# An attention, gated-convolution and feed-forward kernel on one core: new load order, nine opening products, one ring of five accumulator banks, and a new instruction list

## The chip, the core and the metric

The program runs on one core of a Trainium2 chip. The core has five engines with their own instruction streams: TensorE (PE in the profile, with its weight loads as PEld), VectorE (DVE), ScalarE (ACT), GpSimd (POOL) and SyncE (SP), which here only issues transfers. Each engine takes its instructions in the order in which they were written; between engines, semaphores order the work. The metric is device time in microseconds (us) of one execution, as a median over runs.

## The reference, cut to what matters

```python
# q, k, v: (2, 8, 768, 64); attention with a window of +-15 positions and 24 block summaries
k_sum = k.reshape(B, H, nb, 32, D).max(axis=3)          # 24 blocks of 32 keys: maximum
v_sum = v.reshape(B, H, nb, 32, D).mean(axis=3)         # and mean of the values
scores_l = where(|i - j| < 16, scale * q @ k.T, -1e9)
scores_s = scale * q @ k_sum.T + log(32)
a = softmax(concatenate([scores_l, scores_s]))
x = a @ concatenate([v, v_sum])                          # -> (2, 768, 512)
h = relu(x @ w_in)                                       # 512 -> 1024
gate = sigmoid(conv3(h, conv_w))                         # along the sequence, by channel
x = (h * gate) @ w_out                                   # 1024 -> 512
xn = (x - mean) / sqrt(var + 1e-6) * g_ln
out = x + relu(xn @ w_ch1) @ w_ch2                       # 512 -> 2048 -> 512
```

The weights arrive as 64-bit floats. They are loaded as raw 32-bit words and narrowed on the chip in three steps (`...z` on VectorE, `...b` on ScalarE, `...c` on VectorE), then split into a high part (`...d`, ScalarE) and a remainder (`...e`, GpSimd), because the big products are made as three reduced-precision products: high by high, high by low, low by high.

## The kernel before

The program is a list of 1850 operations, each a small function that emits a few instructions. `plan.op` declares an operation with the engines that it may run on, what it comes after, and what it takes from a ring of buffers. The string `ORDER` names all operations by number in the order in which they are emitted, with the letter of the chosen engine (V, A, G, P, S); so it decides both the order on every engine and which engine does a movable operation. The numbers of nanoseconds in `plan.op` are only notes for whoever made the list: they emit nothing.

The work in order of time:

- **Attention** over 12 pairs j of 64-row windows (6 per batch). For a pair, `M` writes a mask into two banks of scores (units 2j and 2j+1), `S{j}` adds the products of queries and keys, `X` takes the row maximum (VectorE), `E` the exponentials (ScalarE, four ACTIVATE instructions), `Q` and `R` the reciprocal of the row sums, `N` the normalisation (GpSimd or VectorE), `P` the transposes, `C` their copy out, `T{j}` the value products, and `H{j}`, `L{j}` the copy of the result into a high and a low part of `xT`. Before that, keys and queries are transposed (`kt`, `kb`, `qt`), copied out (`kn`, `qe`), and the block maxima of the keys taken (`kmb`). The scores of the first batch need the maxima of all three blocks of 256 keys (`k0`, `k1`, `k2`), which `kc` copies into the key tiles.
- **The gated convolution** in 48 steps i: `h{i}` are 12 products (a group of 8 steps for each 256 rows), `r` the relu (ScalarE, it frees the bank of h), `b`, `c` the convolution, `t`, `g` the gate, `u`, `v` its high and low part (ScalarE, GpSimd), and `x{i}` six products, up to about ten steps behind h. The first of them, `h0`, waits for `L0`, `L1` and, through two columns that `xh1` copies, `L2`.
- **The feed-forward part**: `ch` (12 products) and `ac` (three products each into six accumulators), over both batches, about from 215 us to the end.

TensorE writes into eight banks of an accumulator memory (PSUM). `PS` divides them until the attention is through: tag `tr` 2 banks (transposes), `sc` 2 (scores), `av` 1 (value products), `h` 1, `x2` 2 (x, and in the opening also key transposes and block means of v). A tag is a ring: a request gets the bank of the request that lies as many requests back as the ring is long, and waits until that one is read out.

```python
PS = {"tr": (ps_a, 2), "sc": (ps_a, 2), "av": (ps_a, 1), "h": (ps_m, 1), "x2": (ps_m, 2)}
```

All loads are issued by SyncE in list order. The opening order before: conv weights, a block of `w_in`, `k2`, `w_in`, `k1`, `k0`, `w_in`, `q0`, two blocks of `w_in`, `q1`, and so on; each block of k, q, v, and weights is 512 KB. The program begins with six products on a zeroed tile (`warm_up`) whose result nobody reads.

## Time and profile before

| | |
|---|---|
| median of three runs | 497.84 us (497.32 to 498.03) |
| the profiled execution | 497.72 us, span 496.0 us from the first to the last instruction |
| TensorE busy | 478.9 us, 97% of the span |
| VectorE, ScalarE, GpSimd busy | 306.5, 225.7, 149.6 us |
| granted TensorE clock, mean | 1.00 |

The page shows TensorE busy in nine tenths or more of every fortieth of the span but the first three (6, 8 and 8 tenths), the fourth (7) and the last (6). VectorE is at nine tenths or nearly so in the first six slices, and the transfers fill the first eight. In the second half VectorE, ScalarE and GpSimd are mostly idle and TensorE never is. Bars of this kind tell where an engine has room; they don't tell what the program's end hangs on, which is read from the waits.

### The profile page before, as it was taken

How to read it: one execution, taken by the hardware profiler on the slowest of the kernel's cores; microseconds unless marked ns; L12 is line 12 of the kernel's file. 1: busy time of each engine (PE TensorE's matmuls, PEld its weight loads, DVE VectorE, ACT ScalarE, POOL GpSimd, SP SyncE). 2: the span in 40 equal slices, each digit the busy share in tenths (PEclk: the TensorE clock that was granted, in tenths of full speed). 3: DMA queues.
4: the chain of work that ended last, by engine and by line, in shares of the span. 5: the costliest groups of instructions: out<-in, count | busy, mean ns of one | idle time of the engine just before them, and what ended most of it. 6: DMA issues, size and time to landing. Idle time of an engine off the chain costs nothing.

```text
span 496.0 us, 8646 instructions
## 1 busy us (share of the span) xinstructions
PE 478.9 (97%) x3342; PEld 417.3 (84%) x3342; DVE 306.5 (62%) x600; ACT 225.7 (46%) x601; POOL 149.6 (30%) x183
## 2 busy tenths in 40 slices
PE   6887999999999999999999999999999999999996
PEld 4646888888889888887999898998899889998985
DVE  4998989877677898999999931251463011410114
ACT  3897978666755586755453402340153001110110
POOL 4776555634643244415432000330044000000000
PEclk9999999999999999999999999999999999999999
DMA  8999998201110225000635000422022000300003
GB/s 253 347 261 258 240 180 161 60 1 34 30 34 1 88 85 169 1 1 9 213 119 163 8 0 1 170 86 85 1 87 83 0 1 0 128 0 2 0 1 127
DMA packets 60136, 43.26 MB, mean 87 GB/s; under 512 B 34324, under 2 KB 55088, under 8 KB 60096
## 3 DMA queue, kind: packets, MB, share of 16 engines
q1 hardware_dynamic: 59952, 42.58, 31.2%
q8 instruction: 26, 0.43, 0.4%
q14 instruction: 14, 0.11, 0.1%
q10 hardware_dynamic: 144, 0.13, 0.1%
HBM read 39.22 MB, written 3.15 MB: 85 GB/s over the span
## 4 chain that ended last, share of the span: by engine, by line
PE 81%; DVE 6%; DMA 6%; SPq 2%; ACT 2%; issue 1%; POOL 1%; DVEq 0%; ACTq 0%; POOLq 0%
PE ch L1112 27%; PE acc L1147 26%; PE h L704 10%; PE x L776 10%; PE av L489 2%; DMA s_k<-in_k_dram 2%; DVE c L732 2%; DMA vw<-in_v_dram 2%; PE sc L473 1%; PE tr L567 1%; DMA raw<-in_moe_w_ch_dram 1%; PE tr L351 1%; DMA early<-in_k_dram 1%; SPq L662 1%; DVE g L745 1%
## 5 line engine op out<-in xcount | busy, mean ns | idle before, releaser
L1147 PE MATMUL acc<-wh,ch 128*128 128x512 f32 x382 | 126.2, 394 | 0.7 <-ACT x2b L252 0.7
L1123 DVE SCALAR_TENSOR_TENSOR ch<-ch,ch 128x384 fp32r<-128x384 f32 x64 | 35.1, 555 | 133.7 <-ACT ch L1119 133.6
L1112 PE MATMUL ch<-xnT,wh 128*128 128x384 f32 x512 | 99.8, 336 | 0.0
L1119 ACT ACTIVATE ch<-ch 128x384 fp32r<-128x384 f32 x64 | 30.8, 491 | 150.5 <-PE ch L1112 101.8
L1112 PEld LDWEIGHTS ch<-xnT,wh 128*128 128x128 f32 x512 | 90.6, 188 | 3.5 <-DVE ch L1123 0.2
L1147 PEld LDWEIGHTS acc<-wh,ch 128*128 128x128 f32 x382 | 71.6, 188 | 16.4 <-ACT x2b L252 1.1
L704 PE MATMUL h<-xT,wi 128*128 128x258 f32 x576 | 82.9, 288 | 1.2 <-ACT h L716 1.1
L704 PEld LDWEIGHTS h<-xT,wi 128*128 128x128 f32 x576 | 75.5, 189 | 9.1 <-ACT h L716 5.9
L645 POOL TENSOR_TENSOR wl<-raw,wh 128x512 fp32r<-128x512 f32 x32 | 43.0, 1364 | 117.9 <-ACT wh L643 94.0
L1147 PE MATMUL acc<-wl,ch 128*128 128x512 f32 x191 | 75.0, 393 | 0.0
L776 PE MATMUL x<-wo,ghi 128*128 128x512 f32 x192 | 61.5, 401 | 0.0
L763 POOL TENSOR_TENSOR glo<-g,ghi 128x256 fp32r<-128x256 f32 x48 | 39.7, 836 | 62.7 <-ACT ghi L756 52.8
L732 DVE SCALAR_TENSOR_TENSOR c<-h,ccol,c 128x256 f32<-128x256 f32 x96 | 51.2, 544 | 7.9 <-POOL c L256 4.6
L1112 PE MATMUL ch<-xnT,wl 128*128 128x384 f32 x256 | 54.9, 336 | 0.0
L1112 PEld LDWEIGHTS ch<-xnT,wl 128*128 128x128 f32 x256 | 45.3, 188 | 0.0
L1147 PEld LDWEIGHTS acc<-wl,ch 128*128 128x128 f32 x191 | 35.8, 188 | 6.7
L776 PE MATMUL x<-wo,glo 128*128 128x512 f32 x96 | 37.9, 394 | 0.0
L1082 DVE STREAM_TRANSPOSE xf<-xn 32x384 f32<-32x384 f32 x64 | 36.4, 569 | 1.2
L776 PEld LDWEIGHTS x<-wo,ghi 128*128 128x128 f32 x192 | 32.3, 189 | 4.1 <-issue 0.3
L538 ACT ACTIVATE prob<-sc,nm 128x120 f32<-128x120 f32 x96 | 33.2, 370 | 2.7 <-DVE nm L526 2.7
L643 ACT CAST wh<-raw 128x512 fp32r<-128x512 f32 x32 | 19.9, 662 | 24.0 <-PE acc L1147 13.7
L628 ACT ACTIVATE raw<-raw 128x512 f32<-128x512 f32 x32 | 20.6, 677 | 17.8 <-DMA raw<-in_moe_w_ch_dram 17.8
(129 smaller groups left out, 584.1 us busy)
## 6 DMA issues: line engine op xcount, KB each, us to landing
raw<-in_moe_w_ch_dram SPq DMA_DIRECT2D x32, 512.0 KB, 4.8
wst<-in_moe_w_out_dram SPq DMA_DIRECT2D x8, 512.0 KB
vw<-in_v_dram SPq DMA_DIRECT2D x20, 192.0 KB, 4.7
wst<-in_moe_w_in_dram SPq DMA_DIRECT2D x5, 512.0 KB
s_q<-in_q_dram SPq DMA_DIRECT2D x8, 256.0 KB, 6.5
early<-in_k_dram SPq DMA_DIRECT2D x3, 512.0 KB, 8.0
x2a<-in_moe_w_in_dram SPq DMA_DIRECT2D x3, 512.0 KB
early<-in_v_dram SPq DMA_DIRECT2D x3, 512.0 KB, 6.1
```

The source lines that it names most:

```text
L538: A.activation(out=pr[:, p, :], in_=sc[:, p * NK:(p + 1) * NK], func=AF.Exp, bias=nm[:, p:p + 1], scale=1.0, accum_out=sm[:, p:p + 1])
L628: A.activation(out=f, in_=f, func=AF.Prelu, scale=F64_SCALE, alpha=F64_SIGN)
L645: lambda e: G.tensor_tensor(out=lo(), in0=narrowed(raw()), in1=hi().bitcast(F32), op=ALU.subtract),
L704: T.matmul(live["h", i][:, 0:CH + 2], w_[:, c, f * 128:(f + 1) * 128], x_[:, c, :], start=(k_ == 0 and c == 0), stop=(k_ == 2 and c == 3))
L732: V.scalar_tensor_tensor(out=ct, in0=ht[:, kk:kk + CH], scalar=ccol[:, kk * NF + f:kk * NF + f + 1], in1=ct, op0=ALU.mult, op1=ALU.add)
L763: on[e].tensor_tensor(out=glo, in0=live.pop(("g", i)), in1=live["ghi", i].bitcast(F32), op=ALU.subtract)
L776: T.matmul(x2ps[g, t], l[:, ts_], r[:, f, :], start=(f == 0 and j == 0), stop=(f == NF - 1 and j == 2))
L1082: V.transpose(out=o_, in_=i_)
L1112: T.matmul(cp[:, 0:384], w_[:, c * 128:(c + 1) * 128], x_[:, c, s], start=(n_ == 0), stop=(n_ == 11))
L1119: A.activation(out=chs[b, m][0][:, s], in_=live[key][:, 0:384], func=AF.Relu)
L1123: V.scalar_tensor_tensor(out=lo[:, s], in0=live.pop(key)[:, 0:384], scalar=0.0, in1=hi[:, s].bitcast(F32), op0=ALU.max, op1=ALU.subtract)
L1147: T.matmul(acc[key], l[:, ts_], r[:, 512:1024], start=(mm == 0 and j == 0), stop=(done and j == 2))
```

## The change

Six things change; what the kernel computes stays. (1) `ORDER` is a new list, so nearly every engine's order moves, and 87 operations move to another engine: among them 10 normalisations `N` go from GpSimd to VectorE and 2 the other way, 4 query copies from ScalarE to VectorE and 4 back, 3 key copies from ScalarE to VectorE. (2) The first loads are `k0`, `k1`, `k2`, then a block of `w_in`, the conv weights, `w_in`, `q0`, two of `w_in`. (3) `warm_up` has nine products in place of six. (4) The banks `tr`, `sc` and `av` become one ring `tr` of five. (5) The h of odd steps up to 11 takes its bank from that ring too, so that consecutive h have different banks. (6) The release of the attention's memory waits for these relus as well (`HR`); they lie far ahead of it. The changed nanosecond notes emit nothing.

```diff
-4G 0V 8S 61S 12S 73S 11S 1P 178G 228G 3G 2G 10S 52V 157G 53A 6G 54V 7G 67S 63A 62V 5G 64V 13S 36P 79S 33P 37A 75A
...
+1834P 1845V 1846P 1849V 1847V
...
-    PS = {"tr": (ps_a, 2), "sc": (ps_a, 2), "av": (ps_a, 1), "h": (ps_m, 1), "x2": (ps_m, 2)}
+    PS = {"tr": (ps_a, 5), "h": (ps_m, 1), "x2": (ps_m, 2)}
...
-        for _ in range(6):
+        for _ in range(9):
...
-            tag = SCT.get(u, "sc")
+            tag = "tr"
...
-            av = live["av", j] = bank("av")
+            av = live["av", j] = bank("tr")
...
-        ex.give.append((SCT.get(i, "sc"), ("s", i)))
+        ex.give.append(("tr", ("s", i)))
...
+        htag = "tr" if i % 2 and i < 12 else "h"
...
-                    live["h", i] = bank("h")
+                    live["h", i] = bank(htag)
...
-    lk = {n: dma(f"lk{n}", 1456, load_pairs("k", k, 0, n, early_at(0, n))) for n in range(3)}
+    lk = {n: dma(f"lk{n}", 1650, load_pairs("k", k, 0, n, early_at(0, n))) for n in range(3)}
...
-    gate2 = list(XL.values())
+    gate2 = list(XL.values()) + HR
```

TensorE's order in the opening. Ahead of these rows stand the six, now nine, opening products. `L358` are transposes of keys and queries (in `before` k2, k1, k0, then q0 and q1), `L465` (now `L464`) the masks, `L473` (`L472`) the score products, 32 for a pair, `L821` (`L823`) the block means of v, `L567` (`L566`) the transposes of the probabilities. Before, from the key transposes on:

```order
L358 MATMUL x_195<-ident,early_83 64x128 x8
L358 MATMUL x_210<-ident,early_83 64x128 x8
L358 MATMUL tr<-ident,early_83 64x128 x16
L358 MATMUL x_250<-ident,early_83 64x128 x8
L358 MATMUL tr<-ident,early_83 64x128 x8
L473 MATMUL sc<-kw_86,qb_89 64x120 x16
L358 MATMUL tr<-ident,early_84 64x128 x16
L821 MATMUL x_338<-early_84,ind 24x512 x2
```

And now:

```order
L358 MATMUL x_254<-ident,early_83 64x128 x8
L358 MATMUL tr<-ident,early_83 64x128 x8
L472 MATMUL tr<-kw_86,qb_89 64x120 x32
L823 MATMUL x_332<-early_84,ind 24x512 x2
L848 MATMUL x_346<-ident,crow 128x28
L823 MATMUL x_332<-early_84,ind 24x512 x2
L566 MATMUL tr<-ident,prob 120x128 x8
L823 MATMUL x_332<-early_84,ind 24x512 x2
L358 MATMUL tr<-ident,early_84 64x128 x16
```

Before, the first pair's scores (`S0`, whose equal instructions the view counts as x16) stand alone, and q1 is transposed right behind them; now four masks are written early and `S1` and `S0` stand together (x32), with the transposes of q1 (`early_84`, 16) behind the first two probability transposes. What stands before `h0` is the same set of TensorE operations in both lists.

ScalarE's order from the first exponentials (`L538`, now `L537`) on. `L628`/`L643` (`L627`/`L642`) are the narrowing and the high part of a block of weights, `L252` copies out of banks. Before:

```order
L538 ACTIVATE prob,sm<-sc,nm 128x120 x8
L628 ACTIVATE wst<-wst 128x512
L628 ACTIVATE x2a<-x2a 128x512
L643 CAST wi_81<-wst 128x4x128
L643 CAST wi_81<-x2a 128x4x128
L628 ACTIVATE wst<-wst 128x512
L538 ACTIVATE prob,sm<-sc,nm 128x120 x8
L252 COPY probT<-tr 120x512
L252 ACTIVATE vsum<-x_338 24x512
```

And now:

```order
L537 ACTIVATE prob,sm<-tr,nm 128x120 x4
L642 CAST wi_81<-wst 128x4x128
L537 ACTIVATE prob,sm<-tr,nm 128x120 x8
L627 ACTIVATE x2a<-x2a 128x512
L642 CAST wi_81<-x2a 128x4x128
L627 ACTIVATE wst<-wst 128x512
L252 COPY probT<-tr 120x512
L252 ACTIVATE vsum<-x_332 24x512
L537 ACTIVATE prob,sm<-tr,nm 128x120 x4
```

Three of the first four exponentials now come together and the fourth after three weight steps and two copies; from the first exponential to the copy `H2` that `h0` needs, ScalarE has 8 exponentials, 8 weight steps and 9 copies before, and 8, 12 and 11 now.

## Rows read from the trace of the kernel before

**Rows 1.** Stretches: busy PE, PEld, DVE, ACT, POOL; clock, DMA share, GB/s.

```profile
0.00:10.00 10.00, 5.94 (x36) 3.97 (x38) 3.26 (x7) 3.45 (x5) 4.70 (x25) 1.00 0.79 242
...
30.00:40.00 10.00, 7.47 (x118) 4.59 (x117) 9.91 (x21) 8.68 (x34) 7.77 (x7) 1.00 1.19 200
...
300.00:350.00 50.00, 50.00 (x256) 45.68 (x255) 13.80 (x24) 14.20 (x26) 10.36 (x8) 1.00 0.25 85
```

**Rows 2.** What TensorE waited for, longest first: us in total, times, longest.

```profile
PE x L358 <- DMA early<-in_k_dram: 3.0, 1, 3.0
PE tr L567 <- POOL prob L557: 2.3, 3, 1.4
PE av L489 <- DVE parts L951: 1.4, 1, 1.4
PE sc L465 <- ACT prob L538: 1.3, 3, 0.8
PE sc L473 <- ACT kw L252: 1.2, 1, 1.2
PE h L704 <- ACT h L716: 1.1, 2, 0.9
...
PE acc L1147 <- ACT x2b L252: 0.7, 1, 0.7
PE tr L351 <- DMA s_k<-in_k_dram: 0.6, 1, 0.6
```

**Rows 3.** Timeline of TensorE's opening: start, duration, operation, wait before it.

```profile
1.04 2.74 PE L277 MATMUL h<-warm 128*128 128x512 bf16 x6 [1.04 <-DVE warm L272]
...
6.79 1.97 PE L358 MATMUL x<-ident,early 128*64 128x128 f32 x16 [3.01 <-DMA early<-in_k_dram]
...
8.53 1.95 PE L358 MATMUL tr<-ident,early 128*64 128x128 f32 x16
...
16.65 1.09 PE L358 MATMUL tr<-ident,early 128*64 128x128 f32 x16
...
18.93 1.05 PE L473 MATMUL sc<-kw,qb 64*64 64x120 f32 x32 [1.19 <-ACT kw L252]
...
25.38 1.05 PE L473 MATMUL sc<-kw,qb 64*64 64x120 f32 x32
```

**Rows 4.** Timeline of the other engines in the opening.

```profile
0.79 0.42 SPq L791 DMA_DIRECT2D craw<-in_moe_conv_w_dram  x1
...
1.27 0.41 SPq L662 DMA_DIRECT2D wst<-in_moe_w_in_dram  x1
...
5.20 0.69 ACT L628 ACTIVATE wst<-wst 128x512 f32<-128x512 f32 x1 [2.48 <-DMA wst<-in_moe_w_in_dram]
...
15.92 1.28 DVE L379 TENSOR_REDUCE ksum<-tr 128x16 f32<-128x512 f32 x2
```

**Rows 5.** Timeline of ScalarE from its first exponential.

```profile
22.19 0.36 ACT L538 ACTIVATE prob<-sc,nm 128x120 f32<-128x120 f32 x1
...
23.55 0.37 ACT L538 ACTIVATE prob<-sc,nm 128x120 f32<-128x120 f32 x1
...
37.00 1.12 ACT L252 COPY probT<-tr 120x512 f32<-120x512 f32 x2
...
45.47 0.59 ACT L252 CAST xT<-av 128x512 fp32r<-128x512 f32 x1
45.96 1.28 ACT L628 ACTIVATE wst<-wst 128x512 f32<-128x512 f32 x2
```

**Rows 6.** Timeline of TensorE: the first h.

```profile
47.50 1.72 PE L704 MATMUL h<-xT,wi 128*128 128x258 f32 x12
```

**Rows 7.** GpSimd beside VectorE, then L633's durations (ns: least, median, longest).

```profile
13.89 1.56 POOL L645 TENSOR_TENSOR wi<-wst,wi 128x512 fp32r<-128x512 f32 x1 [0.72 <-ACT wi L643]
14.55 1.45 DVE L633 SCALAR_TENSOR_TENSOR wst<-wst 128x512 uint32<-128x512 uint32 x1 [0.25 <-ACT wst L628]
...
L633 DVE SCALAR_TENSOR_TENSOR wst<-wst x13: 666/690/1451, 5.9 to 80.6; 128x512 uint32<-128x512 uint32 x13
```

More of the change, by code (lines that the diff above doesn't have):

```diff
@@ L275, in warm_up @@
         wb = bank("h")
-        for _ in range(6):
+        for _ in range(9):
             T.matmul(wb.rearrange("p (a b) -> p a b", a=4), warm, warm.unsqueeze(1).to_broadcast([128, 4, 128]),
                      start=True, stop=True)
-    w0_ = plan.op("warm", (("P", 2990),), warm_up, [wz], take=[("h", "warm")])
+    w0_ = plan.op("warm", (("P", 3843),), warm_up, [wz], take=[("h", "warm")])
     w0_.give.append(("h", "warm"))
@@ L490, in f_av @@
                                  ps[a][:, p, 64 * h_:64 * h_ + 64], start=True, stop=True)
-        tt = T_[j] = plan.op(f"T{j}", (("P", 1090),), f_av, cs + [LV[j], LVS[j]], take=[("av", j)])
+        tt = T_[j] = plan.op(f"T{j}", (("P", 1090),), f_av, cs + [LV[j], LVS[j]], take=[("tr", ("av", j))])
         for a in range(2):
@@ L666, in weight @@
         prev = j - 6 if j in (6, 7, 8) else j - 3 if j > 8 else None
-        l = dma(f"lw{j}", 1456, ld, WD[prev] if prev is not None else [])
+        l = dma(f"lw{j}", 1800, ld, WD[prev] if prev is not None else [])
         if j < NF:
@@ L707, in m_step @@
                            ([waits[0]] + waits[2:] if k_ < 2 else waits) + [prev],
-                           take=[("h", i)] if k_ == 0 else [])
+                           take=[(htag, ("h", i))] if k_ == 0 else [])
         H_[i] = prev
@@ L790, in local_summary_attention_moe_kernel @@
     craw = at.tile([24, 256], F32, name="craw")
-    lc = [dma("lc0", 70, lambda: nc.sync.dma_start(out=craw.bitcast(U32),
+    lc = [dma("lc0", 300, lambda: nc.sync.dma_start(out=craw.bitcast(U32),
                                                    in_=conv_w.rearrange("k (f p) -> (k f) p", p=256))),
           dma("lc1", 10, lambda: nc.sync.dma_start(out=crow[24:28], in_=g_ln.rearrange("(c p) -> c p", p=128)))]
-    lk = {n: dma(f"lk{n}", 1456, load_pairs("k", k, 0, n, early_at(0, n))) for n in range(3)}
-    lq = {0: dma("lq0", 1456, load_pairs("q", q, 0, 0, early_at(0, 3))),
-          1: dma("lq1", 1456, load_pairs("q", q, 0, 1, early_at(1, 3)))}
-    lvp = {n: dma(f"lvp{n}", 1456, load_pairs("v", v, 0, n, early_at(1, n))) for n in range(3)}
+    lk = {n: dma(f"lk{n}", 1650, load_pairs("k", k, 0, n, early_at(0, n))) for n in range(3)}
+    lq = {0: dma("lq0", 1650, load_pairs("q", q, 0, 0, early_at(0, 3))),
+          1: dma("lq1", 1650, load_pairs("q", q, 0, 1, early_at(1, 3)))}
+    lvp = {n: dma(f"lvp{n}", 1650, load_pairs("v", v, 0, n, early_at(1, n))) for n in range(3)}
     for n in range(NCH):
@@ L895, in f @@
             stage["q", m] = t
-        return dma(f"lq{m}", 2912, f, take=[("s_q", m)])
+        return dma(f"lq{m}", 2700, f, take=[("s_q", m)])
     def k_keep(m, ld):
@@ L945, in ld @@
                                       :, hf * 1024:(hf + 1) * 1024])
-            l = dma(f"lvb{i}", 1092, ld, take=[("s_k", ("vb", i))])
+            l = dma(f"lvb{i}", 1850, ld, take=[("s_k", ("vb", i))])
             def f(e, i=i, raw=raw):
@@ L1207, in local_summary_attention_moe_kernel @@
     with tc.manual_schedule():
-        plan.trace(list(XL.values()))
+        plan.trace(gate2)
         ps_a.release()
```

186 lines of the change are left out of this document (94 added, 92 removed).

## The prediction, on record before the run

> **What bounds the kernel now.** I read the stretches first. Late in the program TensorE is busy 50.00 of 50 us [rows 1]: there only its own work counts, and the change alters no count of it outside the warm-up. Early it is different: from 30 to 40 us TensorE is busy 7.47 of 10 while VectorE has 9.91 and ScalarE 8.68 [rows 1]. So the attention's start is bound by the two engines that read the banks out, and TensorE waits for what they finish.
>
> The list of TensorE's waits says how much there is to win [rows 2]: 3.0 us for the first keys, then 2.3, 1.4, 1.3 and 1.2 behind normalisation, value sums, exponentials and key columns, and 1.1, 0.7 and 0.6 for the bank of h, the copy of the last x and a late key load. That is 11.6 us in all. The opening of TensorE shows the first keys at 6.79, the first pair's scores at 18.93 and the second pair's at 25.38 [rows 3]; ScalarE begins its exponentials at 22.19 [rows 5]; the first h comes at 47.50 [rows 6]. Both lists have the same TensorE operations ahead of the first h. So the end moves by two things alone: the time at which the first h starts, and the waits behind it.
>
> **The opening, step by step.** The end of the profiled execution is 497.72 us, 1.72 beyond its span of 496.0 and 0.12 below the median, 497.84.
>
> *Keys.* The first weight block was issued at 1.27 and was there at 5.20 [rows 4], 3.93 later; `k2`, behind it, was there at 6.79 [rows 3], 1.6 later. `k0` is now issued first, at the 0.79 of the conv weights [rows 4], so it lands at about 4.7, and `k1` at 6.3. Nine opening products take 1.5 times the 2.74 us of six [rows 3] and end at about 5.0: they fill the wait, and cost 0 to 0.3 us. TensorE starts on keys 1.8 us earlier.
>
> *Pace of TensorE.* Sixteen transposes took 1.97 and 1.95 us at 6.79 and 8.53, and 1.09 at 16.65 [rows 3]. This is the slower of the two levels (1.2 GHz) and then the faster (2.4 GHz), although the granted clock stands at 1.00 for 0 to 10 us [rows 1]; ahead of the slow ones TensorE had stood idle for 3.0 us. With the gap filled, the faster level may come earlier: between nothing and 0.9 us on each of the blocks behind the first. I count half of one block, since VectorE takes over next. The Trainium skill (TensorE: Matmul & The Clock Gate, Part 1) says that the clock is throttled by default and that activity releases it. By that page all blocks but the first would run at the faster level, and what VectorE then sees is some 1 us earlier; no run here has shown it.
>
> *VectorE to the first scores.* From the end of the second sixteen transposes, at about 5.0 + 1.95 + 1.5 = 8.4, VectorE's list has nine whole-bank operations (five maxima, two key copies, two query copies) and eight smaller ones (two weight blocks, the conv weights, the key columns). Two maxima take 1.28 [rows 4], so nine take 5.8; for the smaller ones I take an estimate of 0.5 us each, the largest being 0.69 [rows 7], so 4.0. With 0.5 for two waits on TensorE the scores can start at 18.7, range 17.7 to 19.2. That is where the first pair was (18.93), but now both pairs run, the second 6 us earlier than at 25.38 [rows 3].
>
> *ScalarE to the first h.* Two maxima follow weights and key edges, about 3 us after the scores' start; the first exponential begins at 21.7 where it was 22.19 [rows 5]. From there to the copy `H2` ScalarE has 8 exponentials of 1.36 (22.19 to 23.55), 12 weight steps of 0.64 (two in 1.28) and 11 copies of 0.56 (two in 1.12) [rows 5]: 10.9 + 7.7 + 6.2 = 24.8 us. Before it was 10.9 + 5.1 + 5.0 = 21.0, in the 23.9 us from 22.19 to the end of `H2` at 46.06 [rows 5]; 2.9 us were waits. So four weight steps and two copies have moved ahead of `H2`, and eat what the denser start gives. With no wait at all `H2` ends at 46.5, with as many waits as before at 49.4. I take 0.5 us of waits, because the exponentials of two pairs are ready together: 47.0. Before, 1.44 us lay between `H2` and h (46.06 to 47.50); with the same, the first h starts at **48.4, 0.9 us later** than now (range 47.0 to 50.5). VectorE's four normalisations ahead of that point lie inside this, unless they are stretched (below).
>
> **Behind the first h.** A later h moves everything behind it one for one. What can be won back is in the waits there [rows 2]: 1.1 for h's bank, 0.7 in front of the first accumulation, 0.6 for the key load, and perhaps 0.4 of the 1.3 of scores.
> - 0.7: the new list puts three `ch` (36 products) between the last x and the first accumulation, so the copies that it waited for are covered. I count all of it.
> - 0.6: `k4` is now loaded first of the second batch's keys, and fewer value rows stand ahead of it. All of it.
> - 1.1: the bank that alternates is lent only up to step 11, and these waits can fall at any step. I count half, 0.55.
> Moved operations elsewhere (the convolution's steps between engines, key edges between VectorE and GpSimd) lie under TensorE's work; with that cover gone each would cost its own 0.2 to 0.8 us once. The five-bank ring costs nothing by itself.
>
> **Sum.** 497.72 + 0.9 - 0.7 - 0.6 - 0.55 = 496.8, less 0.1 for the scores' wait: **496.7 us**. What a measurement of this kernel can tell from no change is about 0.2%, 1.0 us: 496.84 to 498.84.
>
> **Rivals.**
> - *A full gain.* If the faster clock comes at once and ScalarE waits for nothing, the first h starts at 47.0, 0.5 earlier, and all 2.4 us behind it go: 497.72 - 0.5 - 2.4 = 494.8; with the other score waits 494.3. For it: ScalarE's 2.9 us of waits before came from serial pairs. Against: it has 3.8 us more work there.
> - *No change.* The opening is 0.9 later and the late waits change place: with half of 2.4 us won, 497.4, with none 498.6. For it: in the late stage VectorE is still needed for each step, and the list gives it more.
> - *Slower: the ring's order.* In one ring a request waits for the request five back. The second query transpose of q1 gets the bank of the first pair's masks, which is read out only by `E0`, now the fourth exponential; behind it on TensorE stand the probability transposes and `S2`, `S3`. I have `E0` end at 31; each us later moves `S2`, the next exponentials and the first h by a us. If `E0` is 2.5 us late, the first h is at 50.9, and the end is 497.72 + 3.4 - 1.4 = 499.7. It decides from about 1.5 us on. For it: `E0` is behind a maximum that is behind a normalisation and a weight step on VectorE, each waiting for another engine. Against: the others of this ring are free in time by my sums.
> - *Slower: normalisations on VectorE.* A VectorE operation with two operands from the data memory, begun at 14.55 beside GpSimd's of 13.89 to 15.45, took 1.45 where the median is 0.69 [rows 7]. The four normalisations now on VectorE ahead of `L2` meet GpSimd's weight steps; at up to 0.76 each they cost up to 3.0, half of it on the path: 498.2. The Trainium skill (SBUF, Who interferes with whom) gives the rule: VectorE instructions with two inputs there are blocked by a GpSimd instruction that reads it, for its whole length. This row agrees in part: the longest was lengthened by 0.76, not by the full 1.56.
> - *The opening products miss.* If `k0` lands at 5.7, not 4.7, the gap returns and 0.5 to 1 us is lost: 497.4. It is within the case of no change.
>
> **Chances.** My forecast with its own spread (495.6 to 497.8) 0.42; full gain 0.14; no change or a missed warm-up 0.18; the ring's order 0.16; the normalisations 0.10. Faster by over 0.2%: about 0.6 of the forecast and all of the full gain, 0.40. Slower: the ring, and 0.4 of the normalisations and of no change, 0.28. Same 0.32. The range of 8 in 10 leaves out the best of the full gains and the worst of the ring: 494.2 to 500.2.
>
> **What would show each step.** Right: the first key transposes at 4.7 to 5.1 with no wait for `k`; sixteen transposes at about 1.1 us from the third block on; the first scores, 64 products together, at 17.7 to 19.2; the first exponential at 21 to 22.3; the first h at 47 to 50; the 0.7 before the first accumulation and the 0.6 for the key load gone. Wrong: a wait of a us or more of the q transposes for `E0`; normalisations on VectorE above 1 us; new waits of TensorE for VectorE between 190 and 230, where the late list is tight.

## The result: slower, and the profile after

The changed kernel took **503.84 us** (median of four runs, 502.24 to 504.76) where the kernel before took 497.93 in the same comparison (497.32 to 498.76): a ratio of **1.011, 95% interval 1.0073 to 1.0146**. The forecast was 496.7, in a range of 494.2 to 500.2. The profiled execution took 504.22 us, with a span of 502.5 and a mean granted clock of 0.99.

What TensorE waited for, longest first (us in total, times, longest); the rows answer to [rows 2]:

```profile
PE tr L566 <- POOL prob L556: 6.1, 2, 4.3
PE tr L472 <- DVE qb L256: 2.9, 1, 2.9
PE h L704 <- ACT h L716: 2.6, 4, 1.2
PE acc L1149 <- ACT ch L1121: 1.5, 2, 1.3
...
...
PE acc L1149 <- DVE ch L1125: 0.7, 1, 0.7
```

The waits that the prediction counted as gone are gone: 3.0 for the first keys, 0.7 for the copy of the last x, 0.6 for the late key load. What it didn't see stands in their place: 2.9 and 4.3 in the opening, 2.6 where 1.1 was for the bank of h, and 2.2 of `acc` for the relu of `ch`, where there was none.

TensorE's timeline, which answers to [rows 3] and [rows 6]:

```profile
5.24 1.09 PE L358 MATMUL tr<-ident,early 128*64 128x128 f32 x16 [0.29 <-POOL mask_l L294]
...
17.35 2.57 PE L472 MATMUL tr<-kw,qb 64*64 64x120 f32 x64 [2.92 <-DVE qb L256]
19.85 2.83 PE L823 MATMUL x<-early,ind 128*24 128x512 f32 x4
...
26.48 1.23 PE L566 MATMUL tr<-ident,prob 128*120 128x128 f32 x8 [1.80 <-POOL prob L556]
...
33.91 1.05 PE L472 MATMUL tr<-kw,qb 64*64 64x120 f32 x32
...
41.15 1.11 PE L566 MATMUL tr<-ident,prob 128*120 128x128 f32 x4 [4.31 <-POOL prob L556]
...
43.04 1.98 PE L488 MATMUL tr<-probT,vw 120*64 120x64 f32 x32
...
51.13 1.70 PE L704 MATMUL h<-xT,wi 128*128 128x258 f32 x12 [0.82 <-POOL xT L254]
```

The opening is as forecast down to the first scores, and even earlier: keys at 5.24, the fast pace at once (1.09 for sixteen), scores at 17.35. Then the gain is lost. The third pair's scores (`S2`, 33.91) stood at 31.59 before:

```profile
31.59 1.05 PE L473 MATMUL sc<-kw,qb 64*64 64x120 f32 x32
```

and the first h at 51.13 is 3.6 us later than in [rows 6]. On the way some operations take nearly twice their time: the fifth pair's probability transposes 1.11 (four took 0.65 elsewhere), 32 value products 1.98 (1.15 before). The stretches show why (busy PE, PEld, DVE, ACT, POOL; clock, DMA share, GB/s):

```profile
18.40:21.70 3.30, 3.30 (x35) 1.62 (x28) 3.20 (x7) 1.37 (x6) 1.19 (x1) 0.50 1.12 358
...
38.90:45.60 6.70, 4.45 (x43) 4.01 (x44) 4.64 (x14) 5.04 (x24) 2.46 (x3) 0.50 0.97 293
```

The granted clock, 1.00 through all of [rows 1], falls to 0.50 twice, each time around an idle stretch of TensorE: after the wait of 2.92 that ends at 17.35, and during the 4.31 that end at 41.15. That is the slower of the two levels, 1.2 instead of 2.4 GHz. The 1.00 of [rows 1] for 0 to 10 us is not a measured clock: the trace's first record of it is a rise to 1.00, at 12.09 us in the kernel before and at 4.70 now, and the view counts the time ahead of the first record as 1.00. The transposes of 1.97 in [rows 3] lie before that rise.

Behind the first h, the same view for three stretches, after and then before:

```profile
60.00:90.00 30.00, 29.28 (x288) 24.40 (x287) 28.93 (x55) 24.17 (x68) 19.26 (x22) 1.00 0.73 161
90.00:250.00 160.00, 158.24 (x1274) 138.03 (x1273) 142.97 (x305) 100.89 (x295) 61.72 (x76) 1.00 0.19 55
250.00:340.00 90.00, 87.65 (x435) 77.62 (x434) 51.08 (x89) 27.73 (x52) 16.20 (x12) 1.00 0.22 70
```

```profile
60.00:90.00 30.00, 29.40 (x244) 25.45 (x243) 27.23 (x54) 23.48 (x59) 16.57 (x21) 1.00 0.86 163
90.00:250.00 160.00, 158.16 (x1266) 138.09 (x1265) 136.41 (x294) 100.92 (x292) 68.87 (x84) 1.00 0.19 58
250.00:340.00 90.00, 90.00 (x454) 81.21 (x453) 51.58 (x91) 28.92 (x54) 16.13 (x13) 1.00 0.25 82
```

From 60 to 250 us TensorE idles as long as before (0.7 and 1.8 against 0.6 and 1.8): the waits that went were replaced. From 250 to 340 it never idled; now it idles 2.35 us. So the 6.5 us between the two profiled executions are **3.6 at the first h and 2.4 between 250 and 340 us**, with 0.5 elsewhere. That is one execution of each. The late part isn't a constant of the list: in eight other runs whose order is the same from 250 to 340 us, TensorE idled 0.6 to 1.8 us there (*six_products* 1.84, *vr2_gpsimd* 0.99, *fill_three* 0.82).

Two of these late waits, in the timelines of VectorE, TensorE, SyncE and ScalarE:

```profile
287.90 1.29 DVE L632 SCALAR_TENSOR_TENSOR raw<-raw 128x512 uint32<-128x512 uint32 x2 [0.39 <-ACT raw L627]
289.11 0.55 DVE L1125 SCALAR_TENSOR_TENSOR ch<-ch,ch 128x384 fp32r<-128x384 f32 x1
...
289.71 0.72 PE L1149 MATMUL acc<-wh,ch 128*128 128x512 f32 x2 [0.69 <-DVE ch L1125]
...
328.88 0.37 SPq L1044 DMA_DIRECT2D raw<-in_moe_w_ch_dram  x1
...
335.87 1.20 ACT L627 ACTIVATE raw<-raw 128x512 f32<-128x512 f32 x2 [1.02 <-DMA raw<-in_moe_w_ch_dram]
336.98 0.47 ACT L1121 ACTIVATE ch<-ch 128x384 fp32r<-128x384 f32 x1
...
337.50 0.51 PE L1149 MATMUL acc<-wh,ch 128*128 128x512 f32 x1 [1.30 <-ACT ch L1121]
```

The relu of `ch` (`ca` on ScalarE, L1121; `cv` on VectorE, L1125) is written behind the narrowing of a weight block (L627, L632). The narrowing waits for its transfer or for its neighbour, the relu waits behind it in the queue with its operand long there, and the next accumulation waits for the relu.

### The profile page after: what moved, and what is told of

It reads as the page before. It is cut to its first block, busy times and chain, and to the rows that moved or that the text cites. A ratio compares the mean times of both kernels' runs of the same rounds, so it can differ in the third digit from the quotient of the medians.

```text
span 502.5 us, 8642 instructions
## 1 busy us (share of the span) xinstructions
PE 481.1 (96%) x3345; PEld 417.1 (83%) x3345; DVE 314.4 (63%) x615; ACT 223.7 (45%) x599; POOL 139.6 (28%) x170
## 4 chain that ended last, share of the span: by engine, by line
PE 66%; DVE 14%; DMA 7%; issue 5%; POOL 4%; ACT 2%; SPq 0%; DVEq 0%; POOLq 0%; ACTq 0%
PE acc L1149 21%; PE ch L1114 20%; PE x L778 9%; PE h L704 9%; DMA raw<-in_moe_w_ch_dram 6%; DVE xf L1084 3%; PE tr L488 2%; POOL wl L644 2%; DVE c L734 2%; PE tr L472 2%; PE tr L566 2%; DVE wst L632 1%; DVE raw L623 1%; DVE raw L632 1%; DMA early<-in_k_dram 1%
## 5 line engine op out<-in xcount | busy, mean ns | idle before, releaser
L1125 DVE SCALAR_TENSOR_TENSOR ch<-ch,ch 128x384 fp32r<-128x384 f32 x64 | 35.3, 555 | 130.8 <-ACT ch L1121 130.6
L1121 ACT ACTIVATE ch<-ch 128x384 fp32r<-128x384 f32 x64 | 31.0, 489 | 149.8 <-PE ch L1114 96.7
L704 PE MATMUL h<-xT,wi 128*128 128x258 f32 x504 | 72.3, 287 | 3.4 <-ACT h L716 2.6
L704 PEld LDWEIGHTS h<-xT,wi 128*128 128x128 f32 x504 | 66.1, 189 | 10.1 <-ACT h L716 6.1
L734 DVE SCALAR_TENSOR_TENSOR c<-h,ccol,c 128x256 f32<-128x256 f32 x96 | 54.4, 582 | 3.4 <-ACT c L252 1.7
L537 ACT ACTIVATE prob<-tr,nm 128x120 f32<-128x120 f32 x96 | 33.3, 371 | 6.8 <-DVE nm L525 5.3
L627 ACT ACTIVATE raw<-raw 128x512 f32<-128x512 f32 x32 | 20.6, 678 | 28.5 <-DMA raw<-in_moe_w_ch_dram 28.5
L642 ACT CAST wh<-raw 128x512 fp32r<-128x512 f32 x32 | 20.1, 660 | 18.0 <-PE acc L1149 9.2
```

The lines of the kernel that those rows point to most:

```text
L537: A.activation(out=pr[:, p, :], in_=sc[:, p * NK:(p + 1) * NK], func=AF.Exp, bias=nm[:, p:p + 1], scale=1.0, accum_out=sm[:, p:p + 1])
L627: A.activation(out=f, in_=f, func=AF.Prelu, scale=F64_SCALE, alpha=F64_SIGN)
L704: T.matmul(live["h", i][:, 0:CH + 2], w_[:, c, f * 128:(f + 1) * 128], x_[:, c, :], start=(k_ == 0 and c == 0), stop=(k_ == 2 and c == 3))
L734: V.scalar_tensor_tensor(out=ct, in0=ht[:, kk:kk + CH], scalar=ccol[:, kk * NF + f:kk * NF + f + 1], in1=ct, op0=ALU.mult, op1=ALU.add)
L1121: A.activation(out=chs[b, m][0][:, s], in_=live[key][:, 0:384], func=AF.Relu)
L1125: V.scalar_tensor_tensor(out=lo[:, s], in0=live.pop(key)[:, 0:384], scalar=0.0, in1=hi[:, s].bitcast(F32), op0=ALU.max, op1=ALU.subtract)
```

## Experiments

Ratios are against the kernel before in the same comparison. The list's operations are named as in the section on the kernel before. Filling products are those of the opening, on the zeroed tile into the idle bank of h; nobody reads them.

**1 to 4.** The first four test the clock, the late list, the load on VectorE, and the nine products.

*fill_gaps*, new list:

```diff
+    def fill(n):
+        for _ in range(n):
+            T.matmul(live["wb"].rearrange("p (a b) -> p a b", a=4), warm, ...)
...
         def f_s(e):
+            if j == 1:
+                fill(12)
...
+            if i == 5:
+                fill(16)
             pr, _ = live.pop(("pr", i))
             pt = bank("tr")
```

> The changed kernel, with 12 further products on the zeroed tile ahead of the first scores (S1) and 16 ahead of the transposes P5, where TensorE stood idle for 2.9 and 4.3 us and the granted clock then read 0.5 from 18.36 to 21.77 and from 38.84 to 45.66. Nobody reads their result. Theory: the slow stretch costs time on the path, because P5, the second query transpose, T1, P4 and P6 took 2.1 us more in it than their fast durations; the clock stays at 1.0, the first h comes 1 to 2 us before its 51.13, and the median falls from 503.8 to 502 to 503. Rival: VectorE and ScalarE alone set the first h; then the clock stays up, T1 is shorter, and the first h and the median move by 0.3 us or less.

Measured: 502.16 us, 1.0078 (1.0045 to 1.011). Both filled places run at full clock, but a third gap, a wait of 3.0 ahead of the probability transposes at 25.68, is now followed by the slow level (eight take 1.96, not 1.23); first h at 50.54.

*late_list_before*, new list with the feed-forward operations, in the places that they have there, put into the sequence of the list before:

```diff
 ch, ca, cv, ac, the weight steps y.. and the layer norm:
-  sequence of the new list
+  sequence of the list before, in the same places
```

> The changed kernel, but the operations of the feed-forward part (weights' loads and narrowing, ch, ac, the layer norm and their copies) stand in the order, and on the engines, that the list of before gives them, in the places that the new list gives to such operations. Theory: the four waits of TensorE at 261, 262, 290 and 337 us, 3 us in all, come from that part's new order; they go, and the median falls by 2.5 to 3.5 us to about 500.7. Rival: they come from the later start of everything or from transfers; then they stay, and the median moves by less than 0.7 us. The 0.7 us that the new list won in front of the first accumulation may come back as a wait in either case.

Measured: 516.02 us, 1.0332 (1.0277 to 1.0388). The late waits are gone (none after 257 us), but one h waits 7.6 us for its relu at 210: layer-norm copies that wait for VectorE now stand ahead of it in ScalarE's queue. The run shows how much a place in a queue can cost, and leaves the size of the late waits open.

*vr2_gpsimd*, the value sums `vr2` ahead of the first normalisations moved from VectorE to GpSimd:

```diff
 VectorE:  wi2c cc5
-          vr2
           Q2 Q3
 GpSimd:   N3 N1
+          vr2
           wi4e wi6e
```

> The changed kernel, with one value sum of the second batch (vr2, 1.91 us on VectorE at 23.00, ahead of the reciprocals for which the first normalisations wait) moved to GpSimd behind N1. Theory: VectorE's order is the bound of the opening, since it has no wait of note from 9 to 38 us; so P3 and P2, S2 and P5 all come 1.5 to 1.9 us earlier (S2 at about 32.2 where it was 33.91), the first h at about 49.4, and the median is 1.5 to 1.9 lower, about 502. Rival: ScalarE's amount of work sets the first h, as I had it; then S2 comes earlier but the first h by under 0.5 us, and the median stays.

Measured: 505.61 us, 1.0125 (1.007 to 1.018): a miss. The first transposes came 0.57 us earlier (25.91), but GpSimd took 3.8 us for the sums, the second pair waited (P0 2.67 for VectorE), and the first h came at 54.16.

*six_products*, new list:

```diff
-        for _ in range(9):
+        for _ in range(6):
```

> The changed kernel with six opening products in place of nine; all else as changed. Theory: the nine close the gap ahead of the keys, and so the granted clock reads 1.0 from 4.70 on and sixteen transposes take 1.09 at once; with six a gap of about 1 us opens ahead of the keys, the first blocks take about 2 us each, the first maximum on VectorE comes about 0.9 later, and the first scores at about 18.2 in place of 17.35; the median is 0.5 to 1 us higher, about 504.5. Rival: VectorE's work covers it, and the scores and the median move by less than 0.3 us.

Measured: 503.95 us, 1.0115 (1.0079 to 1.0151), like the changed kernel. Keys at 4.88 after a wait of 1.1, sixteen transposes still 1.09, first h at 50.77. The theory, a slower first block and 0.5 to 1 us more, missed: three products more or less don't move the median. That the early load alone brings the fast pace is not shown, for the pace of the first block differs between executions: with nine products the clock's first rise came at 3.8 to 6.8 us, and the sixteen transposes took 1.09 in the changed kernel, 1.86 in *fill_three* and 1.97 in *chain_first*.

**5 to 8.** Three repairs apart and together.

*chain_first*, new list, `E0` and the second pair's transposes ahead of weight steps:

```diff
 VectorE:
-  N2 wi4c Q1 R1 X0 wi6z C2 wi6c vs1 Q0 R0 wi7z N0 qe11 vs0 wo8z wi7c wo8c X5 X6 X4 Q5 R5 vs2 Q6 Q4 R6 X7
+  N2 X0 wi4c Q1 R1 C2 Q0 R0 N0 qe11 wi6z wi6c X5 X6 X4 wi7z Q5 R5 wi7c wo8z wo8c Q6 Q4 R6 vs1 vs0 vs2 X7
 ScalarE:
-  wi4d wi6b C3 vsum0 E0 qe10 wi6d wi7b C0 C1 wo8b wi7d wo8d E5 E6 E4 qe20 E7
+  E0 wi4d C3 qe10 wi6b C0 C1 wi6d wi7b E5 E6 E4 vsum0 qe20 wo8b wi7d wo8d E7
 GpSimd:
-  wi6e wo8e wi7e N5 N6
+  wi6e N5 N6 wo8e wi7e
 TensorE:
-  vb2 qt10 qt11 P1 M5 P0 M4 M6 S2 M7 S3 qt20
+  qt10 qt11 P1 M5 P0 M4 M6 S2 M7 S3 vb2 qt20
```

> The changed kernel, with another order between 25 and 42 us only: on VectorE the maxima X0, X5, X6, X4, the normalisation N0 and the query copy qe11 stand ahead of the narrowing of weights and of the value rows, on ScalarE E0 and E5, E6, E4 ahead of weights, on GpSimd N5 and N6 ahead of two weight remainders, and on TensorE the transposes of q1 and S2, S3 ahead of the last block mean of v. No operation is added or changes its engine. Theory: the first h is late because S2 and, behind it, the fifth unit's exponential and normalisation stand behind weights in VectorE's and ScalarE's queues; then S2 starts at about 31 (33.91 before this edit), P5 at about 38.3 (41.15), the first h at 48 to 49 (51.13), and the median falls by 2 to 3 us to about 501.5. Rival: the two engines' total work sets the first h, and the weights moved back delay it as much; then S2 and P5 come earlier, but the first h or the steps right behind it don't, and the median stays within 0.7 us of 503.9.

Measured: 505.67 us, 1.0132 (1.01 to 1.0163). TensorE's timeline:

```profile
32.72 1.05 PE L472 MATMUL tr<-kw,qb 64*64 64x120 f32 x32
...
41.86 1.98 PE L488 MATMUL tr<-probT,vw 120*64 120x64 f32 x32 [2.35 <-ACT wo L642]
...
46.78 1.94 PE L566 MATMUL tr<-ident,prob 128*120 128x128 f32 x8 [2.95 <-DVE prob L556]
...
53.97 1.70 PE L704 MATMUL h<-xT,wi 128*128 128x258 f32 x12 [0.16 <-POOL xT L254]
```

`S2` is 1.2 us earlier, as wanted, and the first h 2.8 later: the copies of `vs` that were put off come back as waits (the three take 3.74 us on VectorE from 41.11, beside GpSimd's remainders; 0.65 each alone). The rival was right.

*late_list_cut*, new list up to `ch040` (some 257 us), the rest in the sequence of the list before:

> The changed kernel up to ch of the fifth weight block (about 257 us), and from there on the order and the engines of before's list; at the cut both lists have loads and slots in the same state, so nothing stands ahead of its turn. Theory: the waits at 261, 290 and 337 us (up to 3.0 us in all) are this part's own order; they go, no wait above 0.3 us is left after 257 us, and the median falls by 2 to 3 us to about 501.5. Rival: they come from the landing times of transfers, whatever the order; then waits of the same size stand at other places, and the median moves by under 0.7 us.

Measured: 507.06 us, 1.0162 (1.0133 to 1.0191). The waits at 289 and 337 are gone; two others, 1.6 and 1.8, stand at 263 and 268.

*fill_three* adds a third filling to *fill_gaps*:

```diff
+            if i == 3:
+                fill(10)
             if i == 5:
                 fill(16)
```

> The changed kernel with 12, 10 and 16 further products on the zeroed tile ahead of S1, P3 and P5, in all three of the gaps of 1.8 to 4.3 us (with two filled, the third made the granted clock fall to 0.5 for 3.4 us). Theory: the clock stays at 1.0 throughout, and the first h comes at 49.5 to 50, against 50.54 with two gaps filled and 51.13 with none; the median is about 501.5. Rival: VectorE sets the first h, so that it stays at 50.5.

Measured: 501.75 us, **1.0047 (1.003 to 1.0064)**, an interval below that of the changed kernel. The kernel before took 499.45 in this comparison and 497.93 in that one, so the gain is read more safely from the medians: 2.1 us, and the runs of the two don't overlap (500.82 to 501.97 against 502.24 to 504.76). Its timeline, and the stretch that had the slow clock:

```profile
14.35 2.76 PE L284 MATMUL h<-warm 128*128 128x512 bf16 x12
17.35 1.87 PE L480 MATMUL tr<-kw,qb 64*64 64x120 f32 x64 [0.24 <-DVE qb L256]
...
33.48 1.05 PE L480 MATMUL tr<-kw,qb 64*64 64x120 f32 x32
...
40.75 0.65 PE L578 MATMUL tr<-ident,prob 128*120 128x128 f32 x4 [0.89 <-POOL prob L564]
...
49.49 1.71 PE L716 MATMUL h<-xT,wi 128*128 128x258 f32 x12 [1.21 <-POOL xT L254]
```

```profile
38.90:45.60 6.70, 5.46 (x98) 4.28 (x98) 5.53 (x17) 6.16 (x25) 2.06 (x3) 1.00 0.96 321
```

With work that serves nothing in the gaps the clock stays at 1.00, and the first h is 1.64 us earlier (51.13 to 49.49). In other executions with the same order up to there it came at 50.77 (*six_products*) and 52.01 (*late_list_cut*) without fillings, and at 49.38 (*fill_late*) and 49.24 (*fill_relu_first*) with them: the size is known to about an us, the direction is clear. The fillings take nothing away: TensorE would have waited for the same operations.

*all_mended*: *chain_first*, *late_list_cut* and fillings of 12, 10 and 8 together.

> The three edits together: scores ahead of weights between 25 and 42 us, the list of before from about 257 us on, and 12, 10 and 8 filling products. Theory: the losses are separate and add up; the first h at 47.5 to 48.5, no waits after 257 us, and the median at 497 to 498.5, the time of before. Rival: the losses share a cause, and the sum of the gains is clearly smaller, with a median of 500 or more.

Measured: 506.88 us, 1.0166 (1.0133 to 1.0199); first h at 53.48, a wait of 2.0 at 268. Its clock fell as well (0.52 from 45 to 52 us), behind a wait of 3.8 for a normalisation. The order edits cost more than the clock gives back.

**9 to 12.** Orders again.

*fill_swap*, *fill_three* (fillings 12, 10, 12) with one exchange on GpSimd:

```diff
-  wi6e wo8e wi7e N5 N6
+  wi6e N5 N6 wo8e wi7e
```

> The changed kernel with its clock kept up (12, 10 and 12 filling products ahead of S1, P3 and P5, as in the run with three gaps filled), and one exchange more: on GpSimd the normalisations N5 and N6 stand ahead of two weight remainders that stood ahead of them. Theory: what holds P5 back is that the row sum Q5 on VectorE (1.22 us where others take 0.15) ran beside a weight remainder on GpSimd, and N5 behind it; P5 comes about 1.5 us earlier (40.75 with three gaps filled), T1, T0, T2 and the first h (49.49) follow by 1 to 1.5, and the median is 500.5. Rival: VectorE's total work up to L2 sets the first h; it stays within 0.4 us, and so does the median of 501.75.

Measured: 503.08 us, 1.0117 (1.008 to 1.0155). The fifth pair's transposes came at 39.21, 1.5 us earlier, and the first h at 50.41, 0.9 later than in *fill_three*. Timelines of GpSimd and VectorE:

```profile
43.26 1.48 POOL L656 TENSOR_TENSOR wi<-wst,wi 128x512 fp32r<-128x512 f32 x1
...
43.50 1.26 DVE L553 TENSOR_SCALAR sm<-sm 128x4 f32<-128x4 f32 x1
```

The remainders that were put off now lie beside VectorE's small steps; one of these, 0.15 us elsewhere, took 1.26 and ended with GpSimd's operation. Further on, one h waits 3.6 us for its relu, 1.6 in *fill_three*.

*fill_late*: *fill_three* with the sequence of the list before from `ca060` (some 272 us) on.

> The changed kernel with three gaps filled, and from about 272 us on (ac050) the order and the engines of before's list; the earlier cut at 257 us opened waits of its own of 1.8 and 1.6 us just behind the cut, where maxima and layer-norm copies of the two lists don't match. Theory: the wait at 289 us (0.85 in each run of the new list) and that at 337 us (0 to 1.5) belong to the new order, in which ca and cv of one block stand behind the narrowing of weights whose transfer is still under way; both go, and the median falls by about 1.3 us to 500.4. Rival: new waits behind the cut eat this; the median stays at 501.7 or rises.

Measured: 508.27 us, 1.0212 (1.0172 to 1.0251). SyncE, VectorE and TensorE:

```profile
279.55 0.37 SPq L1056 DMA_DIRECT2D raw<-in_moe_w_ch_dram  x1
...
283.44 0.43 DVE L635 TENSOR_SCALAR raw<-raw 128x512 uint32<-128x512 uint32 x1 [5.08 <-DMA raw<-in_moe_w_ch_dram]
...
286.34 2.93 PE L1126 MATMUL ch<-xnT,wh 128*128 128x384 f32 x8 [5.33 <-DVE ch L1137]
```

One wait of 5.3 us, none behind it. It is the mechanism of the late waits at its largest: VectorE stands at a narrowing whose load was issued 3.9 us before, and the relu stands behind it.

*search_new* and *search_old*: the first 950 operations in another order, sought by moving operations with durations from the traces, in the new kernel (with fillings of 4, 4 and 10) and in the one before.

> The changed kernel with another order of the first 950 operations (up to about 190 us), found by moving single operations within each engine's queue in a small model of in-order queues that takes its durations from these traces; 26 of the copies and normalisations change between VectorE, ScalarE and GpSimd; 4, 4 and 10 filling products ahead of S1, P3 and P5. Theory: the order in the queues sets the first h, and work on VectorE can be put behind it without paying later; the first h comes at 48 to 49 and the median at 498 to 500. Rival: the total work of VectorE and ScalarE decides; what is moved back delays the steps up to 80 us, and the median stays at 501 or more.

> The kernel of before (its rings, its six opening products, its loads' code) with an order of the first 950 operations found in the same way; 29 copies and normalisations change their engine. Theory, as for the new list: if the order in the queues can still gain something, the old rings and the old load order can be improved as well; the first h at 46 to 47 (47.50 before) and the median at 494 to 497, so that neither the ring of five nor the keys ahead of all weights is needed. Rival: the list of before is already as good as VectorE's work allows; the median stays at 497 to 499 or is higher.

Measured: 517.82 us, 1.0416 (1.0383 to 1.0449), with the first h at 54.68; and 510.26 us, 1.0252 (1.0214 to 1.0289), with the first h at 49.80. Both missed. The model has neither the collisions of VectorE and GpSimd nor the clock; that these are what it lacked is likely, but wasn't tested.

**13 to 16.** The late waits, and the work on the engines.

*fill_relu_first*, *fill_three* with four relus of `ch` ahead of what stood before them in the queue:

```diff
 ScalarE:
-  la101 la100 la102 ca040 la103 ca041 y70b
+  ca040 la101 ca041 la100 la102 la103 y70b
-  y101b y100b ca070
+  ca070 y101b y100b
-  y111b y110b ca131
+  ca131 y111b y110b
```

and `cv040`, `cv041`, `cv070`, `cv131` in the same way on VectorE.

> The changed kernel with three gaps filled, and four pairs of operations moved forward in the feed-forward part: the maxima ca and their remainders cv of the fifth block (both halves), the eighth (first half) and the fourteenth (second half) stand on ScalarE and VectorE ahead of the narrowing of weights (or the layer-norm copies) behind which the new list has them. Theory: TensorE's waits at 261, 289 and 337 us come from a ca or cv that stands in its queue behind a step that waits for a transfer; each goes, and of the 3 us that before did not have, 1.3 to 2 are won against the 501.75 of the three filled gaps: about 500. Rival: the narrowing comes late instead, and the next block's products wait for their weights; the median stays at 501.7 or rises.

Measured: 500.91 us, 1.0063 (1.0043 to 1.0084), the lowest median of the new list, though its ratio is no better than that of *fill_three*. None of the waits at 261, 289 and 337 is left. But in *fill_three* only that at 289 was there (first row); those at 261 and 337 had gone without any change of order. One of 0.3 is new (second row):

```profile
288.54 0.72 PE L1161 MATMUL acc<-wh,ch 128*128 128x512 f32 x2 [0.69 <-DVE ch L1137]
...
282.54 0.73 PE L1161 MATMUL acc<-wh,ch 128*128 128x512 f32 x2 [0.30 <-DVE ch L1137]
```

The span is 499.5 against 500.2. That the queue makes the wait at 289 is shown; for the larger one at 337 of the changed kernel it is argued from the timelines above. The gain in time, some 0.7 us, is no larger than the difference between comparisons.

*fill_n_gpsimd* and *fill_copies_scalar*: *fill_three* with `N0`, `N2`, `N4`, `N7` back on GpSimd, and with eight copies (`kn01`, `kn10`, `kc0`, `qe00`, `C2`, `qe11`, `qe21`, `H0`) back on ScalarE.

```diff
-  N0V N2V N4V N7V
+  N0G N2G N4G N7G
```

> The changed kernel with three gaps filled, and the four normalisations N0, N2, N4, N7 back on GpSimd, where before had them; the places in the list stay. Theory A (amount of work): up to the first h VectorE is busy 43.8 us from 8 us on, where it was 40.4 in before; without four normalisations of 0.65, one of them stretched to 1.44, the first h comes 1 to 2.5 us earlier than the 49.49 of the three filled gaps, and the median is at 499.5 to 500.7. Theory B (chains): each of the four stands in a chain from scores to value products, a normalisation takes 1.0 on GpSimd, and GpSimd's weight remainders stand ahead of it; the first h comes at 49.5 to 51.

> The changed kernel with three gaps filled, and eight copies back on ScalarE, where before had them: kn01, kn10, kc0, qe00, C2, qe11, qe21, H0. Theory A (amount of work on VectorE): 8 copies of about 0.6 leave VectorE, which is busy without a break from 9 to 38 us; the scores start 1 us or more before 17.35 and the first h 1.5 us or more before 49.49. Theory B (ScalarE's amount, the sum that I had made): ScalarE gets 4 us more; the scores stay, and the first h comes 1 to 3 us later than 49.49, with the median at 502.5 to 505.

Measured: 502.28 us, 1.0093 (1.006 to 1.0125), first h at 49.75; and 501.22 us, 1.0068 (1.0037 to 1.0098), first h at 49.02. Taking work from VectorE moves the first h by 0.3 one way and 0.5 the other, where theory A had 1 to 2.5 us earlier: the amount of work on VectorE alone doesn't explain it, though the work went to engines of the same chain.

*before_n_vector*: the kernel before with `N0`, `N2`, `N4`, `N7` on VectorE.

> The kernel of before with one thing changed: N0, N2, N4, N7 on VectorE in place of GpSimd, at the same places of its list. Theory A (amount of work on VectorE): 2.6 us more ahead of L2; the first h at 49 to 50 where it was 47.50, and the median 1 to 2.5 us above before. Theory B: a normalisation is shorter on VectorE (0.65 against 1.0), and the first h stays within 0.5 us of 47.50.

Measured: 499.07 us, 1.002 (0.9997 to 1.0044). The first h comes at 51.43, 3.9 later, and the end of the profiled execution only 1.7. Of the 3.9, 1.3 were there at the first scores already (20.23 against 18.93), ahead of any normalisation: the clock's first rise came at 15.22 us, not 12.09. The other 2.6 are theory A's figure, but 32 value products at the slow level (1.98) are among them. What the normalisations cost is not settled by this run. A late first h is not handed on one for one: of the waits behind it, the 0.6 for the key load is gone and h's 0.9 is 0.6.

**17 and 18.** The loads and products without the new list: *before_fill17* has 17 opening products in the kernel before, *before_k2_first* nine, and the load of `k2` first of all.

```diff
-        for _ in range(6):
+        for _ in range(17):
```

```diff
 SyncE:
-  lc0 lw0 lk2 lw2 lk1
+  lk2 lc0 lw0 lw2 lk1
...
-        for _ in range(6):
+        for _ in range(9):
```

> The list, the loads and the banks of the kernel before; its opening has 17 products in place of six, so that TensorE has work until the first keys land (row before: keys at 6.79 after 3.0 us idle, sixteen transposes 1.97). Theory A (the opening is a row of waits behind the first keys): the first 16 transposes take 1.1, VectorE's first maximum begins 0.9 earlier (8.5), the first scores start at 18.0 to 18.3 (18.93), the first h at 46.6 to 47.0 (47.50), and the end is 0.3 to 0.7 earlier: ratio 0.9985 to 0.9995. Rival B (VectorE is held by weight steps whose transfers set the time): the transposes are as fast, but the scores stay at 18.7 to 19.0 and the end within 0.2 us.

> The list and the banks of the kernel before, with the load of k2 ahead of the conv weights and the first weight block, and nine opening products: the change's loads and products in small, without its list. Theory A: keys at about 5.2 (6.79) at the fast pace, VectorE's first maximum at 7.0 to 7.8 (9.42), held a little by the weight block that now lands at about 6.8; first scores at 17.0 to 18.0, first h at 45.8 to 47.0, the end 0.5 to 1.5 us earlier: ratio 0.997 to 0.999. Rival B (the new loads only move the wait from keys to weights): VectorE and ScalarE stand behind the late weight block, first scores at 18.5 or later, end within 0.5 us of before or later.

Measured: 498.39 us, 1.0017 (0.9996 to 1.0038), with sixteen transposes in 1.09 and the first scores at 17.92, the first h at 47.17; and 496.93 us, 1.0001 (0.9977 to 1.0025). TensorE in the second, and its clock in a stretch:

```profile
17.38 1.05 PE L473 MATMUL sc<-kw,qb 64*64 64x120 f32 x32 [1.19 <-ACT kw L252]
...
40.86 1.98 PE L489 MATMUL av<-probT,vw 120*64 120x64 f32 x32 [1.61 <-DVE parts L951]
```

```profile
40.80:43.40 2.60, 2.54 (x35) 2.46 (x36) 0.36 (x3) 0.53 (x2) 0.98 (x1) 0.50 0.92 303
```

The scores are 1.55 us earlier than in [rows 3] and the first h, at 47.79, is 0.3 later. The value products still start 0.85 earlier (41.71 before), wait 1.6 for VectorE's sums, and then run at the slow level: 1.98 where 1.15 was. Theory A was right to the scores and wrong at the end. A filling ahead of these products wasn't tried here.

## Why the prediction was wrong, step by step

**Right.** *Keys* (4.7 forecast, 5.24; 4.88 with six products), the *pace* (1.09 from the first block on; in part luck, since the first block took 1.86 and 1.97 in *fill_three* and *chain_first*), *VectorE to the first scores* (17.35, ahead of the range). ScalarE's count of 24.8 us from the first exponential to the end of `H2` measured 23.95. The 0.7 and the 0.6 behind the first h went. The Trainium skill (TensorE: Matmul & The Clock Gate, Part 1) says that the clock starts throttled and that activity releases it; the trace agrees: its first record of the clock is a rise, at 4.70 us near the end of the opening products, and nine of these took 3.91 where twelve of the same took 2.76 from 14.35 in *fill_three*.

**Wrong: "I take 0.5 us of waits, because the exponentials of two pairs are ready together".** ScalarE waited 4.2 us in that stretch, in seven pieces. The larger ones, with the first exponential and `H2`; the rows answer to [rows 5]:

```profile
20.98 0.36 ACT L537 ACTIVATE prob<-tr,nm 128x120 f32<-128x120 f32 x1 [0.55 <-DVE nm L525]
...
27.58 0.66 ACT L642 CAST wi<-x2a 128x512 fp32r<-128x512 f32 x1 [1.24 <-DVE x2a L632]
...
42.34 0.36 ACT L537 ACTIVATE prob<-tr,nm 128x120 f32<-128x120 f32 x1 [0.98 <-POOL prob L556]
...
45.06 0.59 ACT L252 CAST xT<-tr 128x512 fp32r<-128x512 f32 x1 [0.68 <-PE tr L488]
...
48.54 0.59 ACT L252 CAST xT<-tr 128x512 fp32r<-128x512 f32 x1
```

Against the forecast of 48.4 the first h is 2.7 late: the first exponential 0.7 earlier, ScalarE's work 0.85 less, its waits 3.7 more, and 2.0 instead of 1.44 from `H2` to h. The prediction's own upper figure, "with as many waits as before 49.4", was the better choice; `H2` ended at 49.13.

**Wrong: the clock was priced only as something to win.** Around the two waits of 2.9 and 4.3 us TensorE came down to the slow level, and this made part of ScalarE's waits (0.68 of them for value products that took 1.98). Filling took 1.64 us from the first h: that share of the 3.6 is shown, to about an us.

**Open: the other 2 us of the first h.** In *fill_three* `S2` is 1.9 later than before (33.48 to 31.59) and from there to the first h it takes as long as before (16.0 against 15.9). `S2` stands on TensorE behind the transposes of `P0`, and `P0` behind `E0`, the fourth exponential, as the ring rival had it by its rows, though the ring didn't hold anything up: the query transposes for which it feared ran without a wait from 29.46 to 31.43, while `E0` was still reading (30.07 to 31.42). But an earlier `S2` doesn't mend it. In *chain_first* and *before_k2_first* it came 1.2 and 1.4 earlier than in their base and the first h came later; in each list another queue was next, and the clock fell too. Nor, by runs 14 and 15, is it the amount of work on VectorE alone; run 16 leaves that open. Which order would keep the gain isn't settled.

**Wrong: "there only its own work counts", and "a later h moves everything behind it one for one".** The forecast behind the first h was 1.95 won; measured 2.87 lost (from the first h to the end 453.09 us, 450.22 before). The 0.7 and 0.6 were won and given back by h's waits (2.6 against 1.1). The 0.55 counted for the lent bank had no ground even in the trace of the kernel before, where both of h's waits lie far behind step 11, at the 43rd and the last of the 48 steps:

```profile
198.69 1.71 PE L704 MATMUL h<-xT,wi 128*128 128x258 f32 x12 [0.87 <-ACT h L716]
...
216.98 1.72 PE L704 MATMUL h<-xT,wi 128*128 128x258 f32 x12 [0.28 <-ACT h L716]
```

Nor does the lent bank keep h from waiting in the changed kernel: at 54.85 the relu that frees the other bank stands on ScalarE behind an exponential and a weight step. Most of the rest is the 2.35 us between 250 and 340 us, the new list's queues by the timelines, of a kind that the prediction gave "its own 0.2 to 0.8 us once" and put at nothing in the sum. That TensorE was busy for 50.00 of 50 us there [rows 1] was a fact of the list before, not of the stage.

**The rivals.** The normalisations on VectorE met GpSimd once (1.44 instead of 0.65), and it was a normalisation of GpSimd, not a weight step. The row of [rows 7] agrees with the rule better than the prediction says: GpSimd's operation had 0.90 us left when VectorE's began, and 0.76 was lost. The opening products didn't miss. No rival came near 503.84; the highest was 499.7. Each priced one loss, and several came together.

## What to carry to other kernels

A busy share of 100% belongs to an order of instructions; when the order is replaced, each wait in front of each transfer has to be counted anew, and first those instructions that stand in a queue behind one that waits for a transfer. A stretch that is won at the start of a chain over four engines is worth what the next queue leaves of it: follow it to the operation that the end hangs on before counting it. And an idle stretch of TensorE can cost twice, once as the wait and once as slow operations behind it; here useless products in three gaps gave the second part back.

## What the runs showed of the hardware that was not expected

The granted clock fell to 0.50 in the middle of a dense program: from 18.4 us, one us after work had begun again behind 2.92 idle, and from 38.9 within a wait of 4.31. In *before_k2_first* it fell without any wait above 1.6 us: TensorE was busy for 0.91 of the 2.6 us from 38.0 to 40.6. With fillings it was 1.00 throughout (*fill_three*). The same wait doesn't always bring it down. In *late_list_cut*, whose list is that of the changed kernel up to 257 us, the first scores ran at full speed behind their wait, and the fall came with the next one, at 25.9 us:

```profile
17.18 1.87 PE L472 MATMUL tr<-kw,qb 64*64 64x120 f32 x64 [2.89 <-DVE qb L256]
```

Nor does it belong to the new list: in *fill_three*'s comparison the mean clock of the kernel before lay between 0.986 and 1.00 over ten executions, and it was 0.986 to 0.990 in the four of the changed kernel.

A small operation of VectorE can lose most beside GpSimd. In the changed kernel (GpSimd and VectorE):

```profile
38.07 1.29 POOL L644 TENSOR_TENSOR wi<-wst,wi 128x512 fp32r<-128x512 f32 x1
...
38.17 1.22 DVE L545 TENSOR_SCALAR sm<-sm 128x4 f32<-128x4 f32 x1 [0.42 <-ACT prob L537]
```

The same step takes 0.15 us at 40.09. Here and in *fill_swap* it ended within 0.03 us of GpSimd's operation. The Trainium skill (SBUF — State Buffer, Who interferes with whom) says that where VectorE, in a mode that uses two ports, and GpSimd want the pair of ports that they share, the one that issues first has it for its whole instruction; it names `tensor_scalar` among the operations that can enter such a mode. The two rows agree to the end. The first of them lies in the chain to the transposes that TensorE awaited for 4.31 us, so at most 0.7 us of that wait came from it (GpSimd, free at 39.36, began the normalisation behind it at 40.08); ahead of the first h, eight operations of VectorE are lengthened in this way in the changed kernel and eight in the one before.
